# A routed feed-forward phase whose program order is written out by hand on four engines

## The chip, the cores and the metric

The kernel runs on one core of a Trainium2 chip. The time is device microseconds (us) of one execution; for the kernel before it is the median of three runs. A core has five instruction streams that matter here: TensorE (PE, matrix products), VectorE (DVE), ScalarE (ACT), GpSimd (POOL), and SyncE (SP, which here only issues transfers). Each stream runs its instructions in the order in which the built program holds them, and waits on semaphores for the others.

## The reference

The input of the second half is the output of the first: a gated linear attention over 4 batches, 8 heads, 768 steps with 48 channels, whose output is laid out as 3072 rows of 384. Then a mixture of 8 experts, each of which takes exactly 384 rows:

```python
logits = x @ w_gate
flat = logits.flatten()
order = np.argsort(-flat)
for idx in order:
    tok, e = (int(idx) // E, int(idx) % E)
    if assigned[tok] >= 0 or counts[e] >= cap:
        continue
    assigned[tok] = e
    counts[e] += 1
for e in range(E):
    mask = assigned == e
    h = np.maximum(x[mask] @ w1[e], 0.0)
    out[mask] = h @ w2[e]
```

The assignment is greedy over all 24576 logits in falling order, so which expert a row goes to depends on which experts are already full.

## The kernel before

**Two phases.** The attention takes the first 136 us or so. It also computes the logits, every row's best expert, and the rows `x_dram` in HBM from which the experts gather. All its engines follow an order written out by hand (L431), and the change leaves it as it is. The feed-forward phase is everything behind it.

**Routing, one expert at a time.** The kernel does not sort. It finds which expert fills up first and at what logit: `search` (L573) is a search over the bits of that logit in five levels of 7, 7, 6, 6 and 6 bits. A level is a chain through two engines. DVE builds a table `cmp` that compares 3072 digits with all digit values (`compare`, L550), PE adds it up per expert with 24 small products into `rt` (L599, "counts"), DVE compares the counts with what each expert may still take (`g`, L600), PE adds these flags up (L606), DVE takes the maximum `k` (L608) and the next digit `nd` (L611). After the fifth level the full expert `es` is known, and `weights` (L526) has SP load its two weight matrices, 3 MB in four transfers. Two small products (L632, L633) give running offsets, `extract` (L704) makes a one-hot table `hot` (L721), PE turns it into row numbers (24 products, L733), DVE writes `idx` (L735), and POOL issues three indirect transfers of 128 rows each into `xr` (L740). `update` (L641) then takes the full expert out and gives each row its next best choice: `top`, the first table of the next search, `chu`, `o`, `rem`. Seven of the eight experts are searched for; the last is what is left (`search_last`, L683).

**The products.** They are done in pairs of rounded float32 pieces. `split` (L757) has ACT write the upper part `whi` of a block of weights and POOL the rest `wlo` (L768); a block is 128 of the 1024 hidden columns, seven blocks of buffers are there. `prep` (L778) turns the gathered rows on PE (L792), ACT keeps the upper part `xh` (L795), DVE the rest `xl` (L797). `ffn1` (L802) is nine products of 128x384 into `h` (L808), followed by `hh` on ACT (L812) and `hl` on DVE (L813); `ffn2` (L818) is nine products into three `y` tiles (L828). So each expert has 144 products, 72 in each half, and the phase 1152. The last block's `y` goes through ACT to `yt` (L832) and POOL scatters it to the output (L839), three indirect transfers per expert.

**What sets the order around the change.** In the feed-forward phase the kernel before does not fix the order. The loop at L859 declares the work expert by expert, and a scheduler places each instruction on its engine by priority. The kernel steers it with priorities (`route`, L848, runs at high priority) and with `issue_after` edges: transposes of an expert come after block 5 of the previous one (`prep`, L786), and in the first expert after some idle-time products `spin_after` on zeros (L561, counts 6, 4, 2, 2). The lines of `BEHIND` (L15) make a POOL split wait until a certain table of the search is done.

**Positions.** In this text, a position is the number of the 1152 products that PE's stream holds ahead of an instruction.

## Time and profile before

| what | value |
|---|---|
| runs | 444.43, 446.31, 446.60 us, median 446.31 |
| profiled execution | 441.98 us |
| its span, first to last instruction | 440.3 us |
| PE busy | 402.0 us, 91% of the span |
| DVE busy | 285.3 us, 65% |
| POOL busy | 273.8 us, 62% |
| ACT busy | 195.9 us, 44% |
| mean granted TensorE clock | 0.951 |

The profiled execution is 1.7 us longer than its span, and 4.3 us (1.0%) shorter than the median of the runs. The profile has several views: a table of busy time by stretch of the span with the granted clock, the list of waits (which engine waited for whom, total, times, longest), the timeline of one engine with the idle time before a row in square brackets and what ended it, and the chain of work that ended last. Matmuls are pipelined, so a row's duration is longer than the distance from its start to the next start; where a product is priced, it is by that distance.

### The profile page before, as it was taken

Reading aid. Unit: us, or ns where it says so; the run is one execution under the profiler, and the core shown is the slowest. Engines: PE = TensorE matmul, PEld = TensorE weight load, DVE = VectorE, ACT = ScalarE, POOL = GpSimd, SP = SyncE. Lnnn points to the kernel's source line nnn. Section 1 sums busy time; section 2 is a strip of 40 time slices with the busy share of each in tenths; the row PEclk is TensorE's granted clock in tenths of the full one; section 3 lists DMA queues with packets and bytes.
Section 4 is the critical chain, followed back from the end, with each engine's and each line's share of the span. In section 5 each row is a group of like instructions: output and inputs, shape, how many; then the busy total and the mean of one; then the engine's idle time right before and its main releaser. Section 6 shows DMA issues by size and latency. Waiting matters only on the chain.

```text
span 440.3 us, 10854 instructions
## 1 busy us (share of the span) xinstructions
PE 402.0 (91%) x4142; PEld 350.9 (80%) x4142; DVE 285.3 (65%) x838; ACT 195.9 (44%) x447; POOL 273.8 (62%) x303
## 2 busy tenths in 40 slices
PE   7999998989897569997998999999999999899993
PEld 3687776768676439987998899799889889799993
DVE  7788888879636665565677777767668677422210
ACT  2377576556564343144226125315415424545411
POOL 4668988677610062745568766774785786798702
PEclk8599999999999856998999899999999999999999
DMA  8999976660006654092055146127118109910101
GB/s 278 320 262 259 245 207 197 180 194 3 2 3 215 220 192 146 1 312 72 13 186 172 41 131 210 55 91 251 55 46 290 63 6 325 348 56 0 56 2 54
DMA packets 34468, 63.40 MB, mean 144 GB/s; under 512 B 3328, under 2 KB 14592, under 8 KB 34416
## 3 DMA queue, kind: packets, MB, share of 16 engines
q1 hardware_dynamic: 28176, 48.54, 36.0%
q0 software_dynamic: 3072, 9.44, 6.6%
q10 hardware_dynamic: 3168, 4.72, 3.1%
q8 instruction: 33, 0.54, 0.5%
q14 instruction: 19, 0.16, 0.1%
HBM read 53.25 MB, written 9.44 MB: 142 GB/s over the span
## 4 chain that ended last, share of the span: by engine, by line
PE 61%; DVE 12%; issue 8%; DMA 7%; POOL 5%; ACT 4%; POOLq 0%; SPq 0%; ACTq 0%; DVEq 0%
PE h L808 16%; PE y L828 14%; PE rt L599 5%; PE y L310 5%; PE y L304 4%; PE s L255 4%; POOL wlo L768 3%; DMA xr<-x_dram,idx 3%; DVE cmp L550 3%; PE xt L247 3%; PE xt L792 2%; PE st L323 2%; PE st L277 2%; DMA w2r<-in_moe_w_dram 2%; DVE sc L219 2%
## 5 line engine op out<-in xcount | busy, mean ns | idle before, releaser
L768 POOL TENSOR_TENSOR wlo<-w2r,whi 128x384 fp32r<-128x384 f32 x64 | 64.9, 1014 | 26.5 <-DVE cmp L550 25.2
L812 ACT ACTIVATE hh<-h 128x384 fp32r<-128x384 f32 x64 | 31.4, 490 | 96.2 <-PE h L808 94.2
L768 POOL TENSOR_TENSOR wlo<-w1r,whi 128x384 fp32r<-128x384 f32 x64 | 64.7, 1012 | 10.7 <-ACT whi L762 4.7
L740 POOL DMA_INDIRECT xr<-x_dram,idx x24 | 29.3, 1219 | 61.5 <-DVE scr L657 31.1
L828 PE MATMUL y<-wlo,hh 128*128 128x384 f32 x192 | 66.9, 349 | 0.0
L828 PE MATMUL y<-whi,hh 128*128 128x384 f32 x192 | 66.6, 347 | 0.0
L828 PE MATMUL y<-whi,hl 128*128 128x384 f32 x192 | 65.4, 341 | 0.0
L813 DVE SCALAR_TENSOR_TENSOR hl<-h,hh 128x384 fp32r<-128x384 f32 x64 | 35.4, 554 | 41.4 <-ACT hh L812 40.8
L762 ACT ACTIVATE whi<-w1r 128x384 fp32r<-128x384 f32 x64 | 32.2, 522 | 52.9 <-PE y L828 36.4
L267 POOL TENSOR_SCALAR_AFFINE_SELECT sm<-sm 128x512 f32<-128x512 f32 x48 | 29.4, 636 | 32.9 <-ACT sm L263 32.9
L808 PE MATMUL h<-xl,whi 128*128 128x384 f32 x192 | 48.6, 354 | 0.0
L808 PE MATMUL h<-xh,wlo 128*128 128x384 f32 x192 | 47.7, 348 | 0.0
L808 PE MATMUL h<-xh,whi 128*128 128x384 f32 x192 | 46.2, 350 | 1.2 <-ACT xh L795 1.2
L839 POOL DMA_INDIRECT out_dram<-yt,idx x24 | 28.4, 1184 | 27.0 <-ACT yt L832 22.2
L288 ACT ACTIVATE sb<-st,sc 128x48 f32<-128x48 f32 x80 | 24.6, 331 | 36.5 <-DVE st L295 21.2
L550 DVE TENSOR_TENSOR cmp<-nd,iota 128x1536 bf16<-128x1536 bf16 (+4 forms) x32 | 38.2, 1203 | 0.8
L599 PEld LDWEIGHTS <-cmp 128*128 128x128 bf16 x816 | 30.4, 118 | 9.8 <-DVE cmp L550 8.3
L828 PEld LDWEIGHTS y<-wlo,hh 128*128 128x128 f32 x192 | 36.7, 191 | 0.0
L828 PEld LDWEIGHTS y<-whi,hl 128*128 128x128 f32 x192 | 36.6, 191 | 0.0
L808 PEld LDWEIGHTS h<-xh,whi 128*128 128x128 f32 x192 | 34.1, 193 | 3.1 <-ACT xh L795 2.9
L828 PEld LDWEIGHTS y<-whi,hh 128*128 128x128 f32 x192 | 36.5, 190 | 0.0
L599 PE MATMUL rt<-o,cmp 128*128 128x8 bf16 x816 | 32.8, 175 | 3.9 <-DVE cmp L550 3.8
(171 smaller groups left out, 807.7 us busy)
## 6 DMA issues: line engine op xcount, KB each, us to landing
w1r<-in_moe_w_dram SPq DMA_DIRECT2D x16, 768.0 KB, 5.7
w2r<-in_moe_w_dram SPq DMA_DIRECT2D x16, 768.0 KB, 7.6
vt<-in_v_dram SPq DMA_DIRECT2D x24, 256.0 KB, 5.6
x_dram<-xg ACTq DMA_DIRECT2D x6, 768.0 KB, 3.7
raw_a<-in_alpha_dram SPq DMA_DIRECT2D x19, 226.2 KB, 5.8
raw_k<-in_k_dram SPq DMA_DIRECT2D x19, 224.0 KB, 5.4
raw_q<-in_q_dram SPq DMA_DIRECT2D x19, 224.0 KB, 6.1
raw_a<-in_alpha_dram SPq DMA_DIRECT2D x5, 258.5 KB, 5.0
```

The source lines that it names most:

```text
L267: nc.gpsimd.affine_select(SM[s][:, h], SM[s][:, h], pattern=[[0, 4], [1, C]], compare_op=OP.is_ge, fill=0.0, base=0, channel_multiplier=-1)
L288: nc.scalar.activation(SB[s, u][:, :D], St[p], AF.Copy, scale=ac)
L550: x = nc.vector.tensor_tensor(words(dst, nt, js), keyed(d, nt, js), each(iotas[t], nt, js), op=OP.is_ge)
L599: nc.tensor.matmul(cnt, cmp[:, j // U, :, j % U], o[:, j], start=(j == 0), stop=(j == NU - 1))
L740: last_gather[0] = nc.gpsimd.indirect_dma_start(out=XR[i][:, b], out_offset=None, in_=x_dram, in_offset=bass.IndirectOffsetOnAxis(ap=IDX[i ...
L762: nc.scalar.activation(hi[:, 0], a, AF.Copy)
L768: y = nc.gpsimd.tensor_sub(lo[:, h], x, hi[:, h])
L808: nc.tensor.matmul(o, a[:, 0, d], x[:, d], start=(n == 0), stop=(n == 3 * DB - 1))
L812: nc.scalar.activation(hh, o, AF.Relu)
L813: nc.vector.scalar_tensor_tensor(hl, o, 0.0, hh, op0=OP.max, op1=OP.subtract)
L828: F2[i, q] = nc.tensor.matmul(Y[b], a[:, bs], w[:, 1].rearrange("p a b -> p (a b)"), start=(q == 0 and n == 0), stop=(q == FB - 1 and n == 2))
L839: st_ = nc.gpsimd.indirect_dma_start(out=out, out_offset=bass.IndirectOffsetOnAxis(ap=IDX[i][:, b:b + 1], axis=0), in_=yt, in_offset=None)
```

## The change

All of the feed-forward phase after the first search is put under a manual schedule: DVE, PE, ACT and POOL run their instructions in the order in which the code declares them. The functions are cut into steps (`counts`, `reached`, `flags`, `next_digit`, `table`, `find`, `offsets`, `places`, `one_hot`, `index`, `gather`, `take_places`, `gone`, `best_left`, `new_choice`, `left`, `split_hi`, `split_lo`, `rows`, `rows_lo`, `scatter`), and each step gets a position. `products` yields one product after another, and before each product the steps whose position has come are declared. The arithmetic is the same. What else differs: `ffn1` takes its nine products in the order upper-upper, lower-upper, upper-lower, so that `xl` is read last; the first `ffn1` of an expert from the third on is put ahead of the last `ffn2` of its predecessor; the first expert's second and third transposes go to the `y` tiles; there are 26 spin products instead of 14, sixteen of them in one run behind the first row numbers; and each scatter has a one-element memset ahead of it on POOL.

```diff
-WARM_IN_ROUTE = (6, 4, 2, 2)
+SPIN = (16, 0, 4, 3, 3)
+TRI = 11
+HOT = 24
...
     def ffn1(i, q):
...
-        for a, x in ((hi, XH[i]), (hi, XL[i]), (lo, XH[i])):
+        for a, x in ((hi, XH[i]), (lo, XH[i]), (hi, XL[i])):
...
+    def products():
+        units = []
+        for i in range(E):
+            mine = [(ffn1, i, q) for q in range(FB)]
+            for q in range(FB - 2):
+                mine.insert(3 + 2 * q, (ffn2, i, [q]))
+            if i < E - 1:
+                mine += [(ffn2, i, [q]) for q in range(FB - 2, FB)]
+            else:
+                mine.append((ffn2, i, list(range(FB - 2, FB))))
+            if i > 1:
+                units.insert(len(units) - 1, mine.pop(0))
+            units += mine
...
+    def level(base, i, t, xl=None):
+        at(base, counts, t)
+        for b in xl or ():
+            at(base, rows_lo, i - 1, b)
+        at(base, reached, t)
+        at(base + 2, flags, t)
+        if t < nb - 1:
+            at(base + 2, next_digit, t)
+            at(base + 2, table, i, t + 1)
...
+    def found(base, i, end):
+        at(base, find, i)
+        at(base + TRI, offsets, i)
+        at(base + TRI, places, i)
+        at(base + HOT, one_hot, i, 1)
+        at(base + end, index, i)
+
+    def renewed(base, i):
+        at(base, take_places, i)
+        at(base, gather, i)
+        at(base + 1, best_left, i)
+        at(base + 6, gone)
...
+    with tc.manual_schedule(engines={E_.DVE, E_.PE, E_.Activation, E_.Pool}):
+        find(0)
+        offsets(0)
+        places(0)
+        one_hot(0, 2)
+        index(0)
+        take_places(0)
+        gone()
+        spin_more(SPIN[0])
+        gather(0)
+        best_left(0)
+        left(0)
+        new_choice(0)
+        table(1, 0)
+        for q in range(4):
+            split_hi(0, q)
+        for n in range(3):
+            split_lo(0, n)
+        spin_more(SPIN[1])
+        rows(0, 0)
+        counts(0)
+        rows_lo(0, 0)
+        reached(0)
+        spin_more(SPIN[2])
+        rows(0, 1)
+        flags(0)
+        next_digit(0)
+        table(1, 1)
...
+        spin_more(SPIN[3])
+        rows(0, 2)
+        rows_lo(0, 1)
+        rows_lo(0, 2)
+        spin_more(SPIN[4])
+
+        base = 0
+        levels(0, 1, {1: 1, 2: 9, 3: 21, 4: 36}, {})
+        found(39, 1, 37)
...
+        base = 76
+        for i in range(1, E):
+            loose = i > 2
+            offs = {0: 35, 1: 52, 2: 68, 3: 84, 4: 100} if loose else {0: 33, 1: 49, 2: 64, 3: 79, 4: 94}
+            end = 144 if loose else 133
+            renewed(base, i) if i < E - 1 else at(base, gather, i)
+            if i < E - 2:
+                at(base + 8, table, i + 1, 0)
...
+            at(base + 31, rows, i, 0)
+            at(base + (48 if loose else 45), rows, i, 1)
+            at(base + (60 if loose else 57), rows, i, 2)
+            if i < E - 2:
+                levels(base, i + 1, offs, {0: (0,), 1: (1,), 2: (2,)})
+                found(base + offs[4] + 3, i + 1, end - offs[4] - 3)
...
+            if i > 1:
+                for b, p in enumerate((56, 72, 88)):
+                    at(base + p, scatter, i - 2, b)
```

Three places show how the instructions now stand. The first is DVE behind the first expert's row numbers, where the first table of the second search is built (`cmp`, 128x3072). Before:

```order
L661 TENSOR_TENSOR scr<-scr,masks 128x120
L675 TENSOR_TENSOR rem<-rem,rt 128x8
L663 TENSOR_SCALAR top<-scr 128x24
L550 TENSOR_TENSOR cmp_98<-top,iota 128x3072
L797 TENSOR_TENSOR xl<-xt,xh 128x3x128
L666 SCALAR_TENSOR_TENSOR scr<-scr,scale 128x96
L671 TENSOR_TENSOR val<-val,scr 128x192
```

And now:

```order
L753 TENSOR_SCALAR top<-scr 128x24
L775 TENSOR_TENSOR rem<-rem,rt 128x8
L776 SCALAR_TENSOR_TENSOR rem<-scr,rem 128x8
L761 TENSOR_TENSOR val<-val,scr 128x192
L762 TENSOR_SCALAR scr<-asg 128x24
L764 TENSOR_REDUCE ch<-val 128x24
L767 SCALAR_TENSOR_TENSOR scr<-scr,scale 128x96
L769 TENSOR_TENSOR chu<-ch,scr 128x24
L771 TENSOR_TENSOR o<-scr,chu 128x192
L552 TENSOR_TENSOR cmp_98<-top,iota 128x3072
L824 TENSOR_TENSOR xl<-xt,xh 128x3x128
L619 TENSOR_TENSOR g<-rt,rem 128x8
```

The table came ahead of the new choices and now comes behind all of them. Of the `xl` steps only the first stands ahead of the level's `g`.

The second is PE around the first two levels of the fourth search (`y` are the second halves of the products, `h` the first; `xt` the transposes; a group of counts is 24 pairs like the last two rows). Before, the first level's flags and the second level's counts:

```order
L792 MATMUL xt<-ident,xr 128x128 x2
L606 LDWEIGHTS one_83
L606 MATMUL rt<-g,one_83 128x8
L792 MATMUL xt<-ident,xr 128x128
L808 MATMUL h<-xh,whi 128x384 x6
L599 LDWEIGHTS cmp_99
L599 MATMUL rt<-o,cmp_99 128x8
```

And now, in the same search:

```order
L855 MATMUL y_3398<-whi,hh 128x384
L855 MATMUL y_3398<-wlo,hh 128x384
L855 MATMUL y_3398<-whi,hl 128x384
L835 MATMUL h<-xh,whi 128x384 x2
L818 MATMUL xt<-ident,xr 128x128 x3
L835 MATMUL h<-xh,whi 128x384
L835 MATMUL h<-xh,wlo 128x384 x3
L614 LDWEIGHTS cmp_99
L614 MATMUL rt<-o,cmp_99 128x8
```

Before, six products stood between the counts of the first two levels, and some transposes with them; now sixteen do in the third and fourth search, seventeen from the fifth on, and the flags stand two products behind the counts. The transposes are at a fixed place among them.

The third is POOL behind a gather (`xr`), where the split of the weights (`wlo`) and the scatters (`out_dram`) share the engine. Before:

```order
L740 DMA xr<-x_dram,idx 128x384 x3
L768 TENSOR_TENSOR wlo<-w1r,whi 128x384
L768 TENSOR_TENSOR wlo<-w2r,whi 128x384
L768 TENSOR_TENSOR wlo<-w1r,whi 128x384
L839 DMA out_dram<-yt,idx 3072x384 x3
L768 TENSOR_TENSOR wlo<-w2r,whi 128x384
```

And now:

```order
L799 TENSOR_TENSOR wlo<-w1r,whi 128x384
L871 MEMSET apart 1x1
L872 DMA out_dram<-yt,idx 3072x384
L799 TENSOR_TENSOR wlo<-w2r,whi 128x384
L799 TENSOR_TENSOR wlo<-w1r,whi 128x384
L871 MEMSET apart 1x1
L872 DMA out_dram<-yt,idx 3072x384
```

The three scatters stood in one run ahead of the fourth split; now there is one scatter behind the splits of each level.

More of the change, by code (lines that the diff above doesn't have):

```diff
@@ L559, in gla_moe_kernel @@
     last_k = [None]
[L561 to L571 removed]
     def search(i):
         chu, o, dig = st["chu"], st["o"], st["dig"]
[L575 to L577 removed]
+        st["d"] = dig[0]
         for t, bits in enumerate(BITS):
[L579 to L581 removed]
+            if t == 0:
                 g = g0
@@ L638, in search @@
[L638 to L648 removed]
+        st["es"] = es
@@ new lines, in index, with gather @@
+    def index(i):
+        ix = psx.tile([128, NB], F32, name="xt")
+        for j in range(NU):
+            nc.tensor.matmul(ix, st["hot"][:, j // U, :, j % U], st["rhs"][:, j], start=(j == 0), stop=(j == NU - 1))
+        IDX[i] = rw.tile([128, NB], I32, name="idx", bufs=4)
+        st["ix"] = ix
+    def gather(i):
+        nc.vector.tensor_scalar(IDX[i], st["ix"], float(N // 2), None, op0=OP.add)
+        XR[i] = wp.tile([128, NB, Dm], F32, name="xr")
+        for b in range(NB):
+            g = nc.gpsimd.indirect_dma_start(
+                out=XR[i][:, b], out_offset=None, in_=x_dram,
+                in_offset=bass.IndirectOffsetOnAxis(ap=IDX[i][:, b:b + 1], axis=0))
+        for half in second_half:
+            for d_ in half(1):
+                tc.add_manual_dep(d_.ins, g.ins.name,
+                                  mybir.DependencyInfo(mybir.DependencyClass.Sync, mybir.DependencyReason.DATA),
+                                  reason="rows of the first expert before its later weights")
+        second_half.clear()
```

470 lines of the change are left out of this document (250 added, 220 removed).

## The prediction

> **What bounds the kernel now.** I read the clock and busy time by stretch first, since the change touches only what comes after 136 us, then the list of PE's waits, then single engines around the gaps. The page says PE is the bound:
>
> ```profile
> PE 402.0 (91%) x4142; PEld 350.9 (80%) x4142; DVE 285.3 (65%) x838; ACT 195.9 (44%) x447; POOL 273.8 (62%) x303
> ```
>
> The stretches of the feed-forward phase (length, then PE, weight loads, DVE, ACT, POOL busy, then granted clock) show where PE was not at work, or at work on a slow clock:
>
> ```profile
> 150.00:167.00 17.00, 9.38 (x76) 5.81 (x75) 11.87 (x43) 5.45 (x13) 7.46 (x6) 0.55 0.63 190
> 167.00:173.00 6.00, 6.00 (x28) 5.52 (x27) 3.24 (x6) 2.40 (x6) 1.65 (x2) 0.58 0.62 228
> 195.00:206.00 11.00, 7.98 (x43) 7.33 (x42) 6.07 (x16) 6.27 (x16) 6.43 (x7) 0.84 0.38 124
> 206.00:234.00 28.00, 27.74 (x277) 26.10 (x276) 19.36 (x63) 9.16 (x21) 16.49 (x17) 1.00 0.38 134
> 234.00:250.00 16.00, 14.06 (x130) 12.22 (x129) 12.11 (x26) 6.15 (x14) 13.96 (x12) 0.89 0.23 77
> 280.00:330.00 50.00, 48.08 (x450) 44.24 (x449) 36.12 (x110) 17.18 (x37) 36.15 (x35) 1.00 0.30 101
> 330.00:375.00 45.00, 44.12 (x390) 41.28 (x390) 33.73 (x110) 19.51 (x43) 31.03 (x29) 1.00 0.52 173
> 375.00:385.00 10.00, 8.50 (x69) 7.65 (x68) 3.79 (x7) 5.46 (x13) 7.70 (x8) 1.00 0.97 359
> 385.00:433.00 48.00, 47.94 (x277) 46.81 (x275) 10.04 (x18) 18.66 (x41) 29.62 (x31) 1.00 0.09 28
> ```
>
> Length less PE's busy time is 3.0, 0.3, 1.9, 1.9, 0.9, 1.5 and 0.1 us from the third row on, 9.6 us in all. The clock adds to it: at half clock half of the time is lost. Three stretches have it: 167 to 173 (some 2.5 us lost: 6.00 x 0.42), 195 to 206 (11.00 x 0.16 is 1.8, of which part was idle anyway; I take 1.5) and 234 to 250 (16.00 x 0.11 is 1.8; 1.5). Who made PE wait:
>
> ```profile
> PE xt L792 <- DMA xr<-x_dram,idx: 5.6, 4, 2.5
> PE rt L599 <- DVE cmp L550: 3.8, 7, 0.9
> PE xt L792 <- DVE xl L797: 2.2, 4, 0.9
> ```
>
> Gathered rows that come late (the longest, 2.5 us, is the gap at 197), and tables of the search that come late. So PE has about 15 us to win behind 167 us, 9.6 idle, 2.5 and 3.0 on clock, and no more than that without less work for it.
>
> **The change, part by part.** *Prices.* A product at full clock is 1.56/9 = 0.173 us:
>
> ```profile
> 387.72 1.56 PE h L808 x9
> ```
>
> A level costs PE its counts and its flags, by the distances of starts:
>
> ```profile
> 251.51 0.96 PE L599 MATMUL rt<-o,cmp 128*128 128x8 bf16 x24
> 252.33 0.42 PE L828 MATMUL y<-wlo,hh 128*128 128x384 f32 x1
> 252.59 0.34 PE L828 MATMUL y<-whi,hl 128*128 128x384 f32 x1
> 252.77 0.18 PE L606 MATMUL rt<-g,one 128*128 128x8 bf16 x1
> 252.81 0.42 PE L828 MATMUL y<-whi,hh 128*128 128x384 f32 x1
> 253.07 0.34 PE L828 MATMUL y<-wlo,hh 128*128 128x384 f32 x1
> ```
>
> Counts take 0.82, the product behind them 0.26 in place of 0.17, flags 0.04 and again 0.09: 1.03 us a level. None of this work goes away; the change has the same 1152 products, the same searches and gathers. It only moves when they are asked for.
>
> *The start of the phase.* The rows of DVE and PE behind the first row numbers:
>
> ```profile
> 156.14 0.16 DVE L735 TENSOR_SCALAR idx<-xt 128x3 int32<-128x3 f32 x1 [0.27 <-PE xt L733]
> 158.39 0.17 DVE L663 TENSOR_SCALAR top<-scr 128x24 bf16<-128x24 int32 x1
> 158.60 1.76 DVE L550 TENSOR_TENSOR cmp<-top,iota 128x3072 bf16<-128x3072 bf16 x1
> 166.12 0.97 PE L599 MATMUL rt<-o,cmp 128*128 128x8 bf16 x24
> 166.95 1.63 PE L808 MATMUL h<-xh,whi 128*128 128x384 f32 x4
> 169.44 1.76 DVE L550 TENSOR_TENSOR cmp<-nd,iota 128x3072 bf16<-128x3072 bf16 x1
> 184.79 0.23 DVE L614 SCALAR_TENSOR_TENSOR fl<-rt,k,ramp 128x8 f32<-128x8 f32 x1
> ```
>
> Before, the first table was ready at 160.36, but its counts stood behind three transposes and came at 166.12; the next table ended at 171.20, and the expert was found at 184.8. Now eight more steps of DVE come ahead of the table. As an estimate they take 2 us (ten such steps took 2.46 us from 156.14 to 158.60), so it ends at 158.6 + 2 + 1.76, about 162.4; but its counts stand right behind the first transpose and start there, 3.7 us sooner. The next table needs 5.1 us from counts to its end above; with the flags behind four spins instead of five cold products I take 4.4: it ends at 166.8. The remaining levels are 8, 12 and 15 products apart, 1.4, 2.1 and 2.6 us plus 1.03 each, the first of them short of the chain (priced below at 3.3 us), so 3.3 + 3.1 + 3.6, and then three products and flags: the expert is found near 177.5, some 7 us before 184.8. The first product needs the third transpose and moves only from 166.95 to about 165.8. At 177.5 PE has done 39 products and all levels; in the trace it had done 35 and lacked two levels. That is 4 x 0.17 + 2 x 1.03 = **2.7 us**, with the half clock of 167 to 173 already in it.
>
> The bounds of this term come from the clock. If it stays at 0.5 as in the row of 167 to 173, the 2.5 us lost there are lost again and 0.2 remain. The row that speaks for full clock is the gap at 197: PE took up work at 199.81, and the clock per microsecond, 0.60 from 202 to 203 and 1 behind it, came back at 202.8, after 3.0 us without a pause (the rows of 243 and 247 are the edges of the other slow stretch):
>
> ```profile
> 199.81 0.87 PE L792 MATMUL xt<-ident,xr 128*128 128x128 f32 x3 [2.51 <-DMA xr<-x_dram,idx]
> 199.00:200.00 1.00, 0.19 (x1) 0.70 0.46 158
> 202.00:203.00 1.00, 1.00 (x5) 0.60 0.00 0
> 243.00:244.00 1.00, 0.91 (x25) 0.88 0.00 0
> 247.00:248.00 1.00, 0.70 (x4) 0.91 0.00 0
> 155.97 2.08 PE L569 MATMUL h<-warm 128*128 128x384 bf16 x6
> ```
>
> Sixteen spins at 2.08/6 = 0.35 us or a little less are 5 us without a pause, more than that, so I take full clock from 162 us on.
> [...]
>
> *The gaps at 195 and 234.* The first is the second expert's gather, late because its search was. With that search 7 us earlier and the transposes 31 products (5.4 us) behind the row numbers, the rows are there. A later gather shows what 5.4 us has to cover:
>
> ```profile
> 231.54 0.16 DVE L735 TENSOR_SCALAR idx<-xt 128x3 int32<-128x3 f32 x1 [0.19 <-PE xt L733]
> 235.54 0.52 PE L792 MATMUL xt<-ident,xr 128*128 128x128 f32 x3 [0.78 <-DMA xr<-x_dram,idx]
> ```
>
> 4.0 us from `idx` to rows, with weights in flight. The second gap is DVE and POOL in each other's way:
>
> ```profile
> 245.12 2.86 DVE L550 TENSOR_TENSOR cmp<-nd,iota 128x1536 bf16<-128x1536 bf16 x1
> 250.36 0.95 DVE L550 TENSOR_TENSOR cmp<-nd,iota 128x1536 bf16<-128x1536 bf16 x1
> 245.19 1.01 POOL L768 TENSOR_TENSOR wlo<-w2r,whi 128x384 fp32r<-128x384 f32 x1
> ```
>
> A table of 0.95 took 2.86 us while POOL ran splits that three scatters in a row had pushed back. With one scatter behind each level's splits that doesn't come up. I take both gaps as gone: 3.0 + 0.3 + 1.9 idle and 1.5 + 1.5 clock, **8.2 us**. Below, if the rows are late by the 0.78 above in each of seven experts, 5.5 us come back.
>
> *The waits between 280 and 385.* The waits for tables (1.9 + 0.9) are of the same kind; and from 375 on, with the transfers' share at 0.97, the last expert's weights (3 MB) met the gather before. Now the last but one gather stands 12 products ahead of the last expert's search, and the last gather 194 products ahead of its use. **4.3 us**.
>
> *New waits.* A level's chain is set by DVE, which also does `hl` (554 ns in the mean) between the products' halves:
>
> ```profile
> L813 DVE SCALAR_TENSOR_TENSOR hl<-h,hh 128x384 fp32r<-128x384 f32 x64 | 35.4, 554 | 41.4 <-ACT hh L812 40.8
> 248.04 0.96 PE L599 MATMUL rt<-o,cmp 128*128 128x8 bf16 x24 [0.34 <-DVE cmp L550]
> ```
>
> From these counts to the end of the table at 250.36 + 0.95 = 251.31 it is 3.3 us with one `hl` in it. Fifteen or sixteen products and a level are 3.6 to 3.8 us, so they cover it. From the first level to the second the table is the 1.76 us one and an `xl` (about 0.5) stands ahead: 3.3 + 0.8 + 0.5 = 4.6 against 16 x 0.173 + 1.03 + three transposes (an estimate, 0.3) = 4.1: 0.4 us short in five searches, **2 us** of new waits. The bounds: none, if `hl` falls elsewhere; 0.4 at each of the 25 later levels, 10 us.
>
> Spins, memsets and the new order inside `ffn1` I cost at nothing. The spins end by about 161.5 (5 us from 156.3), and the table that PE needs next only at 162.4; were the table there at once, they would cost up to 1 us. The memsets are covered by POOL's idle third, and `xl` last only gives slack. The last scatters, 433 to 440.3, stay.
>
> **The sum.** 2.7 + 8.2 + 4.3 - 2 = 13.2 us off the profile's 441.98: 428.8. The median of the runs is 1.0% above that execution, so I put 446.31 x 428.8/441.98 = **433 us**.
>
> **The rivals.** *(a) The clock stays low at the start.* For it: the wait ahead of the first row numbers, in which the clock fell (0.55 in the row of 150), is still there, and 14 spins did not lift it before. Against: those stood in four runs of 6, 4, 2 and 2. The row of 199 makes it the less likely. [...] It costs the 2.5 us: 435.5.
>
> *(b) The fixed order makes PE wait at each level.* An engine with a fixed order waits where a scheduler would have put something else in between, and 0.4 us at each of 25 levels is 10 us in place of 2: 441. Against: before, the distance was 6 to 15 products, and most levels there had no wait.
>
> *(c) The gaps only move.* If gathers and weights collide at the new place as at 197 (2.5 us in four of seven experts, 10 us) and the clock stays low at the start too (2.5), 0.7 of the 13.2 us are left: 444 to 448, no change. Against: the spacing of 31 products.
>
> *(d) Slower.* One mechanism: the chain of a level is longer than its spacing by 0.7 us at all 25 levels, since each `hl` between two steps of the search must now wait for its product. That is 17.5 us in place of 2, and idle time within a search can let the clock fall as at 244, which cost 1.5. It decides from 0.6 us per level (15.2/25); at 0.7 and with two such falls it gives 452. For it: in DVE's new order two or three `hl` of 0.55 us stand inside each search. Against: by their positions most have their product behind them already.
>
> **How the numbers follow.** The forecast has 0.50, (a) 0.14, (b) 0.15, (c) 0.08, (d) 0.10; 0.03 are for more than I found, such as waits too short to show as idle time (424 or less). The range of 424 to 445 leaves out most of (d), a part of (c) and the last case. A measurement of this kernel tells 0.5% (444.1 to 448.5) from no change. Faster: 0.50 + 0.14 + 0.15 + 0.03 = 0.82; the same: 0.08; slower: 0.10.
>
> **What would show it.** Right: the second search's `fl` at 176 to 179 and PE's first product near 166; no idle row above 1 us for gathers behind 180; full clock from 162 or 165 on and no fall behind it; tables of 0.95 and 1.76 us, none near 2.9; the chain of waits with products at its core to the end. Wrong: waits of counts for `cmp` or of flags for `g` above 5 us in all (b, d); rows of gathers above 4 us in all (c); a clock of 0.5 until 169 or 172 (a).

## The result

| kernel | median | range of its runs | before beside it | ratio, 95% interval |
|---|---|---|---|---|
| changed, first chip | 434.21 us | 433.69 to 435.52 | 446.21 us | 0.974 (0.971 to 0.978) |
| changed, second chip | 434.43 us | 432.73 to 437.54 | 446.09 us | 0.975 (0.971 to 0.980) |
| changed, third chip | 436.23 us | 433.61 to 437.19 | 445.71 us | 0.979 (0.976 to 0.983) |

The change makes the kernel faster by 9.5 to 12 us. The forecast was 433 us. The profiled execution took 433.69 us, its span is 431.8 us, and its mean granted clock is 0.969. So the two profiled executions are 8.3 us apart, 13.2 had been summed. Of the experiments below, two of ten runs of "offsets later" (441.07 and 441.46 us) and one of four of "levels 8 apart" (464.32 us) took over 1.5% longer than the fastest run of the same kernel and are left out of the medians and ranges.

### The profile page after: what moved, and what is told of

Same layout as the page of the kernel before. It is cut to its first block, busy times and chain, and to the rows that moved or that the text cites. A ratio compares the mean times of both kernels' runs of the same rounds, so it can differ in the third digit from the quotient of the medians.

```text
span 431.8 us, 10887 instructions
## 1 busy us (share of the span) xinstructions
PE 396.6 (92%) x4154; PEld 347.8 (81%) x4154; DVE 284.2 (66%) x838; ACT 195.7 (45%) x447; POOL 279.9 (65%) x327
## 4 chain that ended last, share of the span: by engine, by line
PE 62%; DVE 21%; issue 6%; DMA 4%; POOL 3%; ACT 2%; SPq 0%; DVEq 0%; POOLq 0%; ACTq 0%
PE h L835 17%; PE y L855 16%; PE rt L614 6%; PE y L312 4%; PE y L306 4%; PE s L257 4%; DVE ga L226 3%; DVE sc L221 2%; DVE cmp L552 2%; PE xt L344 2%; DVE hot L699 2%; PE xt L249 2%; DMA raw_a<-in_alpha_dram 2%; PE xt L818 2%; PE xt L708 2%
## 5 line engine op out<-in xcount | busy, mean ns | idle before, releaser
L799 POOL TENSOR_TENSOR wlo<-w1r,whi 128x384 fp32r<-128x384 f32 x64 | 69.2, 1082 | 24.1 <-ACT whi L790 22.4
L799 POOL TENSOR_TENSOR wlo<-w2r,whi 128x384 fp32r<-128x384 f32 x64 | 68.0, 1063 | 25.6 <-PE xt L818 9.5
L855 PE MATMUL y<-whi,hh 128*128 128x384 f32 x192 | 64.9, 338 | 0.0
L835 PE MATMUL h<-xh,whi 128*128 128x384 f32 x192 | 47.5, 346 | 0.1
L835 PE MATMUL h<-xh,wlo 128*128 128x384 f32 x192 | 46.0, 344 | 0.0
L835 PE MATMUL h<-xl,whi 128*128 128x384 f32 x192 | 46.0, 344 | 0.0
L872 POOL DMA_INDIRECT out_dram<-yt,idx x24 | 25.0, 1043 | 18.4 <-ACT yt L859 14.6
L835 PEld LDWEIGHTS h<-xh,wlo 128*128 128x128 f32 x192 | 33.8, 189 | 0.0
L552 DVE TENSOR_TENSOR cmp<-nd,iota 128x1536 bf16<-128x1536 bf16 (+4 forms) x32 | 33.1, 1044 | 1.0
L835 PEld LDWEIGHTS h<-xl,whi 128*128 128x128 f32 x192 | 33.6, 189 | 0.0
```

The source lines that it names most:

```text
L552: x = nc.vector.tensor_tensor(words(dst, nt, js), keyed(d, nt, js), each(iotas[t], nt, js), op=OP.is_ge)
L799: y = nc.gpsimd.tensor_sub(lo[:, h], x[h], hi[:, h])
L835: nc.tensor.matmul(o, a[:, 0, d], x[:, d], start=(n == 0), stop=(n == 3 * DB - 1))
L855: nc.tensor.matmul(Y[b], a[:, bs], w[:, 1].rearrange("p a b -> p (a b)"), start=(q == 0 and n == 0), stop=(q == FB - 1 and n == 2))
L872: st_ = nc.gpsimd.indirect_dma_start(out=out, out_offset=bass.IndirectOffsetOnAxis(ap=IDX[i][:, b:b + 1], axis=0), in_=yts.pop((i, b)), in ...
```

## The profile after, beside the profile before

From the page of the changed kernel, the line of busy time and the line of the granted clock over 40 slices:

```profile
PE 396.6 (92%) x4154; PEld 347.8 (81%) x4154; DVE 284.2 (66%) x838; ACT 195.7 (45%) x447; POOL 279.9 (65%) x327
PEclk9699999999999769999999999999999999999998
```

PE is busy for 5.4 us less, although it has twelve more spins. Behind the 15th slice the clock does not fall until PE is done, in the last. Busy time by stretch of the changed kernel (length, PE, weight loads, DVE, ACT, POOL, granted clock, share and GB/s of the transfers):

```profile
150.00:167.00 17.00, 10.23 (x97) 6.57 (x96) 14.20 (x48) 5.60 (x13) 6.10 (x7) 0.80 0.72 227
167.00:173.00 6.00, 5.62 (x71) 4.83 (x70) 4.29 (x11) 0.89 (x3) 4.01 (x5) 1.00 0.38 141
173.00:195.00 22.00, 20.69 (x196) 19.21 (x195) 17.04 (x59) 8.00 (x19) 15.50 (x15) 1.00 0.50 171
195.00:206.00 11.00, 11.00 (x115) 10.11 (x114) 6.83 (x15) 5.16 (x12) 5.63 (x6) 1.00 0.01 1
206.00:234.00 28.00, 26.60 (x246) 24.70 (x245) 22.86 (x70) 10.69 (x25) 19.77 (x19) 1.00 0.38 135
234.00:250.00 16.00, 14.93 (x144) 13.68 (x143) 9.93 (x37) 7.34 (x17) 12.93 (x16) 1.00 0.25 85
250.00:280.00 30.00, 29.58 (x288) 27.35 (x287) 22.05 (x66) 11.98 (x27) 23.51 (x24) 1.00 0.35 122
280.00:330.00 50.00, 49.82 (x455) 46.79 (x454) 38.99 (x117) 20.09 (x45) 35.81 (x34) 1.00 0.47 162
330.00:375.00 45.00, 41.48 (x352) 38.97 (x350) 26.00 (x84) 18.25 (x41) 33.27 (x39) 1.00 0.54 189
375.00:385.00 10.00, 10.00 (x60) 9.75 (x59) 3.05 (x6) 6.32 (x15) 9.43 (x14) 1.00 0.17 62
```

Length less PE's busy time, and what the low clock cost, from 167 us on. The clock of 195 to 250 before is half of the time in which PE was busy at a clock of 0.50: 2.99 us from 199.40 to 202.80 and 3.42 us from 243.76 to 247.18. At that clock products start 0.32 us apart (201.12, 201.44, 201.76, 202.08) against 0.173 at full clock, so 46% of the time is lost, a little less than the half that the table and the prediction take. Of the stretches that the prediction does not show, PE was busy for 22.00 us from 173 to 195 and 30.00 us from 250 to 280.

| stretch | idle before | clock before | idle now | clock now |
|---|---|---|---|---|
| 167 to 195 | 0 | 2.5 | 1.7 | 0 |
| 195 to 250 | 5.2 | 3.2 | 2.5 | 0 |
| 250 to 280 | 0 | 0 | 0.4 | 0 |
| 280 to 385 | 4.3 | 0 | 3.7 | 0 |
| sum | 9.5 | 5.7 | 8.3 | 0 |

15.2 us became 8.3. That is 6.9 of the 8.5 us between the spans; the first product comes 1.3 us sooner (165.65 us against 166.95), which is the rest, to 0.3 or so. So every loss that the forecast wanted gone is gone. What is there now is new: the idle time in the last columns stands at other instructions. PE's waits in the changed kernel (engine, waiting tile and line, what it waited for, total, times, longest), and the rows of PE and DVE that the text speaks of:

```profile
PE xt L708 <- DVE rhs L701: 4.4, 4, 2.9
PE rt L659 <- DVE rts L640: 3.3, 4, 1.3
PE rt L663 <- DVE rts L653: 2.7, 1, 2.7
PE xt L818 <- DMA xr<-x_dram,idx: 1.5, 1, 1.5
PE rt L614 <- DVE cmp L552: 1.3, 3, 0.7
```

```profile
165.65 0.44 PE L835 MATMUL h<-xh,whi 128*128 128x384 f32 x1
185.81 0.34 PE L708 MATMUL xt<-rhs,hot 128*128 128x3 f16 x6 [0.72 <-DVE rhs L701]
213.69 0.16 PE L659 MATMUL rt<-rts,tri 128*128 128x2 bf16 x1 [0.79 <-DVE rts L640]
246.66 0.16 PE L659 MATMUL rt<-rts,tri 128*128 128x2 bf16 x1 [1.07 <-DVE rts L640]
358.19 0.18 PE L663 MATMUL rt<-rts,tri 128*128 128x1 bf16 x1 [2.72 <-DVE rts L653]
```

```profile
178.28 0.23 DVE L628 SCALAR_TENSOR_TENSOR fl<-rt,k,ramp 128x8 f32<-128x8 f32 x1
354.09 0.56 DVE L841 SCALAR_TENSOR_TENSOR hl<-h,hh 128x384 fp32r<-128x384 f32 x1 [1.23 <-issue]
356.42 1.20 DVE L649 TENSOR_TENSOR asg<-asg,chu 128x24 f32<-128x24 f32 x1
357.94 0.19 DVE L653 TENSOR_REDUCE rts<-scr 128x1 bf16<-128x24 f32 x1
```

Waits for tables are down from 3.1 to 1.3 us (the 3.8 us of the kernel before hold 0.7 us of the first search, which has a line of its own now). Waits for gathered rows are down from 5.6 to 2.1: 1.5 ahead of the first product, and 0.6 at 193.06, which this profile puts down to DVE's `rem` and others of the same order to the gathered rows. In their place stand waits for the steps between a search and its row numbers: the running offsets (L659, L663, for `rts`) and the one-hot table (L708, for `rhs`). The first expert's share of these two lines is not new: 1.3 of the 3.3 us and 2.9 of the 4.4, where the kernel before had 1.3 and 3.3. New are 2.1 us for L659 (0.79, 1.07 and 0.22), 1.5 for `rhs` on L708 and 2.7 for L663.

The longest is the last expert's offset at 358: PE has it 20 products behind the last searched expert's row numbers, and DVE gets there 2.72 us later. DVE takes 6.3 us from these row numbers (351.67) to `rts` (357.94). In its chain stand an `hl` that waits for its product (1.23 us without work, until ACT has its `hh` ready at 354.06, and 0.5 of its own) and an addition, `asg`, of 1.20 us.

## The experiments

Twelve runs of ten kernels were made in three jobs, each job on one chip. The kernel before differs from chip to chip (441.81, 446.09 and 445.71 us), so medians are compared within a job. For the first job, in which the changed kernel itself did not run, the kernel "last routing late" is the bridge, since it ran in the first and in the third.

| job | kernel | median | range |
|---|---|---|---|
| 1 | last routing late | 432.44 us | 431.77 to 433.10 |
| 1 | short spins | 436.14 us | 435.30 to 437.60 |
| 1 | scatters in one run | 436.61 us | 436.32 to 437.44 |
| 1 | offsets later | 437.78 us | 434.42 to 440.87 |
| 2 | changed kernel | 434.43 us | 432.73 to 437.54 |
| 2 | last routing late, 16 and 22 spins | 433.21 us | 433.05 to 434.88 |
| 2 | second search late | 445.94 us | 445.05 to 448.95 |
| 2 | levels 8 apart | 457.35 us | 456.00 to 460.79 |
| 3 | changed kernel | 436.23 us | 433.61 to 437.19 |
| 3 | last routing late, again | 432.50 us | 431.47 to 433.76 |
| 3 | last routing late, 16 and 30 spins | 433.05 us | 432.30 to 436.24 |
| 3 | old order in `ffn1` | 434.57 us | 433.60 to 436.12 |

A second yardstick does without medians. In each profile I take the time from the first expert's running offset (the first row of L659) to the second expert's row numbers (L708), "start", and from there to the end of the span, "rest". In the changed kernel's three profiles these are 34.36 and 246.0, 34.34 and 246.0, 36.27 and 246.9 us.

### The last expert's routing, late

```diff
...
-                at(base + 20, offsets, i + 1)
-                at(base + 20, places, i + 1)
-                at(base + 26, one_hot, i + 1, 1)
+                at(base + 40, offsets, i + 1)
+                at(base + 40, places, i + 1)
+                at(base + 46, one_hot, i + 1, 1)
                 end = 40
-                at(base + end, index, i + 1)
+                at(base + 70, index, i + 1)
```

Its gather, transposes and `xl` move 30 products with it.

> Only the last expert's routing is moved: its running offset and places from position 20 to 40 behind the start of expert 7's plan, its one-hot table from 26 to 46, its row numbers from 40 to 70, its gather and transposes 30 products later. Theory (the one new wait that was not priced, 2.72 us of PE for DVE at 358, comes from the position alone): the wait is gone, idle time of PE from 330 to 375 falls from 3.5 us to about 0.8, time 434.2 - 2.7 = 431.5 us (430.8 to 432.3). Rival 1 (the wait only moves to the row numbers or to the gathered rows of the last expert): a row of 1.5 to 3 us for index or for the transposes appears, time 434 to 436. Rival 2 (DVE's chain itself is what is long there, whatever PE does): the products behind it wait for hl or for cmp instead, time 433.5 to 434.5.

It ran again beside the changed kernel:

> The last expert's routing late, the same kernel as in the first experiment, now beside the changed kernel on one chip. Theory (the 2.72 us wait of the last running offset was on the path that sets the end, and of the waits that it leaves behind 0.5 + 0.5 + 0.4 us are new): 1.5 to 2.5 us below the changed kernel, 432.3 where that takes 434.4. Rival (no gain, the first experiment ran on a quicker chip): within 0.7 us of the changed kernel.

It took 432.44 and 432.50 us, in the third job 3.7 below the changed kernel, so a little above the range of the first forecast and more below the changed kernel than the second one had it; rest is 243.9 and 244.1 us against 246.0 to 246.9. The second run's stretch, and the largest wait that is left in it:

```profile
330.00:375.00 45.00, 43.33 (x367) 40.60 (x366) 27.83 (x85) 19.15 (x42) 32.09 (x35) 1.00 0.52 178
360.19 0.52 PE L818 MATMUL xt<-ident,xr 128*128 128x128 f32 x3 [0.53 <-DMA xr<-x_dram,idx]
```

Idle time there is 1.7 us against 3.5: the wait was on the path that sets the end, 2.7 went and about 1 came back in three small pieces. Rival 1 and rival 2 of the first text fall. By rest the gain is 2.0 us against a changed kernel without a fall of the clock and 2.8 against the one of the third job; the 3.7 us between the medians are more than either, and why is not shown. A part is a second price of the wait. In the third job's profile of the changed kernel the clock fell behind it:

```profile
358.00:360.00 2.00, 0.56 (x3) 0.57 (x4) 1.72 (x6) 0.00 (x0) 0.83 (x1) 0.79 0.20 76
360.00:362.00 2.00, 2.00 (x8) 2.00 (x7) 1.86 (x7) 0.00 (x0) 0.00 (x0) 0.50 0.83 300
362.00:364.00 2.00, 2.00 (x13) 1.96 (x12) 1.44 (x4) 1.06 (x3) 0.00 (x0) 0.85 1.05 392
```

It did so in three of six profiles that have this wait at 358 (here, with short spins, and with the scatters in one run), and in neither of the two of this kernel. By the median no other kernel of the study was faster.

### The offsets of every search, later

```diff
-TRI = 11
-HOT = 24
+TRI = 16
+HOT = 29
...
-            end = 144 if loose else 133
+            end = 144 if loose else 138
```

> Only the distance from the end of a search to its running offsets grows, from 11 to 16 products (and with it the one-hot table from 24 to 29, and the row numbers of the third and fourth expert by 5). Theory (the offsets stand too close behind the search, DVE needs about 3 us for them): the waits of offsets (0.79, 1.07 and 0.22 us) go to 0.2 in all, those of the row numbers (0.37 to 0.72, four of them, 1.8 in all) stay where the distance to the offsets is kept and grow by 0.4 each where it shrinks from 25 to 20: 434.2 - 1.9 + 1.2 = 433.5 us (432.5 to 434.2). Rival (the row numbers set the pace, the offsets only take a part of their wait): waits of row numbers grow by as much as those of offsets shrink, 434.2 (433.7 to 435.5).

It took 437.78 us, 5.3 above the kernel with the late last routing, which is 1.6 above the changed kernel if that stands 3.7 above the bridge, as in the third job; rest is 250.0, 4.0 above. The waits for `rts` of L659 did go: of 3.3 us only the first expert's 1.3 are left. Those for `rhs` grew by 0.5 and 0.6 us, near what was forecast. But all that comes later moved by 10 products, and now first halves end right ahead of a level. DVE, then PE, in the sixth search:

```profile
297.66 0.56 DVE L841 SCALAR_TENSOR_TENSOR hl<-h,hh 128x384 fp32r<-128x384 f32 x1 [1.39 <-ACT hh L840]
298.14 0.55 DVE L824 TENSOR_TENSOR xl<-xt,xh 128x384 fp32r<-128x384 f32 x1
298.60 0.15 DVE L619 TENSOR_TENSOR g<-rt,rem 128x8 bf16<-128x8 f32 x1
```

```profile
298.81 0.17 PE L599 MATMUL rt<-g,one 128*128 128x8 bf16 x1 [0.94 <-DVE g L619]
```

`hl` must wait for its products, `xl` and `g` stand behind it, and PE waits 0.94 us for the flags, in three searches alike. Neither the theory nor the rival had this. The rest of the loss is clock: it fell to 0.50 behind waits of 0.98 us (251) and 0.96 (263), and 30 us at a mean of 0.89 from 250 to 280 are 3.3 us. The waits are the mechanism that the prediction's rival (d) named, an `hl` between two steps of the search, and they show that the positions of the changed kernel are good for the place of the halves among them, not for the spacing alone.

The run also takes the 2.72 us wait apart. The last expert's offset stands 20 products behind the row numbers here too, but no `hl` waits in DVE's chain, and `asg` takes 0.17 us:

```profile
357.75 0.15 DVE L713 TENSOR_SCALAR idx<-xt 128x3 int32<-128x3 f32 x1
361.62 0.18 PE L663 MATMUL rt<-rts,tri 128*128 128x1 bf16 x1 [0.47 <-DVE rts L653]
```

From row numbers to `rts` (361.37) DVE takes 3.6 us in place of 6.3, and PE waits 0.47 us. So the position alone was short by about 0.5 us; of the 2.7 us by which DVE's chain is longer in the changed kernel, 1.7 are the `hl` and 1.0 is the long `asg`. Moving the step gave room to a long chain, it did not shorten it: with the late last routing DVE still takes 6.3 us.

### The run of spins, short

`SPIN` begins with 6 in place of 16.

> Only the first run of idle-time products is cut from 16 to 6, so 2 us without a pause instead of 4.2. Theory (the long run lifts the clock before the products start): clock 0.5 to 0.6 until about 172, as in the kernel before, 2.5 us lost and the second search later by as much: 434.2 + 2.5 = 436.7 us (436 to 438). Rival (the clock rises anyway with the counts, transposes and spins that follow, or the lost time is hidden because the tables of the search set the pace there): 434.2 (433.7 to 435), even at a low clock.

```profile
160.00:163.00 3.00, 1.67 (x27) 1.30 (x28) 2.12 (x3) 2.71 (x7) 1.56 (x2) 0.50 0.51 149
163.00:167.00 4.00, 3.91 (x24) 2.40 (x21) 2.38 (x5) 1.65 (x4) 2.32 (x3) 0.65 0.61 190
167.00:173.00 6.00, 5.54 (x68) 4.64 (x69) 4.58 (x12) 0.49 (x1) 3.95 (x4) 1.00 0.38 138
```

The clock stays at 0.5 until near 166 and is at 1.00 from 167 on, not from 172. Start is 34.84 us, only 0.5 longer. The median, 436.14, lies in the theory's range, but not for the theory's reason: rest is 248.0, 2.0 above the changed kernel, with the fall of the clock behind the wait at 358. The median is 3.7 above the late last routing, as the changed kernel's is in the third job, so beyond the 0.5 us no loss from the spins can be seen. The rival holds: the clock rises anyway, and what is lost until 166 hardly delays anything. What lifts it, with PE busy for 3.91 of the 4.00 us from 163 to 167, and whether the loss lies under the table, was not tested apart. So the forecast's reason for the full clock, a run of 5 us without a pause, was not needed.

It was not enough either. The third job's profile of the changed kernel, with its 16 spins:

```profile
168.00:174.00 6.00, 6.00 (x41) 5.07 (x40) 3.05 (x8) 1.10 (x3) 3.17 (x4) 0.50 0.06 19
```

The clock was up (1.00 from 163 to 168) and fell again, for 6 us in which PE had no pause; start is 36.27 us, 1.9 longer. This is so in three of the ten profiles whose first run has 16 spins (36.3 to 36.5 us in the other two, both with the late last routing). The longest wait from 156 us to the fall is 0.87 us, ahead of the counts at 166.09. Why the clock falls in some executions of the same first part and not in others is not shown.

### More spins

On top of the late last routing, 16 spins stand ahead of `index(0)`, and 22 or 30 in place of 16 behind it.

> The last expert's routing late, as in the first experiment, and more idle-time products: 16 in PE's wait for the first row numbers, and 22 in place of 16 behind them. [...] Rival 1 (a low clock is hidden there behind tables and gathered rows): clock 1.0, the time that of the first experiment, 432.4 (431.8 to 433.1). Rival 2 (the longer run of spins ends behind the gathered rows): first product 1 us later or more, 433 to 434.

> As the kernel with the late last routing, with 16 idle-time products in PE's wait for the first row numbers and 30 in place of 16 behind them. With 22 PE stood idle for 1.66 us ahead of the gathered rows, and the clock fell right behind, to 0.5 from 163 to 166. Theory (a wait of 1.5 us or more ahead of products is what lets the clock fall; 30 products at full clock are 4.9 us and reach to the rows): no fall from 152 on, idle time for the gathered rows below 0.6 us, 1 to 2 us below the kernel with the late last routing (430.8). Rival 1 (the clock at the start is hidden behind the tables of the second search): the same as that kernel within 0.7 us. Rival 2 (the long run meets a low clock in many executions and is then 9 us long): 2 to 4 us above it, with a wide spread.

With 22, PE had the rows late and the clock fell right there:

```profile
161.43 0.52 PE L818 MATMUL xt<-ident,xr 128*128 128x128 f32 x3 [1.66 <-DMA xr<-x_dram,idx]
162.00:164.00 2.00, 2.00 (x28) 1.44 (x29) 0.00 (x0) 2.00 (x6) 1.84 (x2) 0.67 0.12 48
164.00:166.00 2.00, 1.99 (x9) 1.26 (x8) 1.46 (x5) 0.67 (x2) 1.09 (x2) 0.50 0.82 222
```

With 30 it did not fall: the profile has a clock of 1.00 from 156 on and a mean of 0.984. But start is 34.94 and 35.30 us, no better than the 34.3 of a changed kernel without a fall, and the times are 433.21 and, beside 432.50 for the same kernel without them, 433.05 us. Rival 1: the clock of this stretch is largely hidden. DVE's chain sets the pace there: with 30 spins and a full clock PE waits for DVE four times, at 161.69, 164.24, 166.73 and 169.72 (0.42, 0.60, 0.47 and 0.38 us). More spins cannot shorten that.

### The scatters in one run

`enumerate((56, 72, 88))` becomes `enumerate((54, 54, 54))`: all three scatters of an expert are issued behind the second level's table, ahead of the splits.

> Only the three scatters of an expert are put in one run again, ahead of the splits of the second level (position 54 in place of 56, 72 and 88). Theory (spreading the scatters is what ended the tables of 2.4 to 2.9 us): POOL's splits run into the next table, a table of 2 us or more and a wait of counts of about 1.5 us appear in each of the four searches that have scatters, and the clock falls in one or two of them: 434.2 + 6 = 440 us (438 to 442). Rival (POOL's spare third takes the run, since its splits now have a place of their own): no table above 1.3 us among those of 128x1536, waits of counts below 1 us in all, 434.2 (433.7 to 435).

From the groups by line and shape, one table in DVE's timeline, PE's wait for it, and the clock later on:

```profile
L552 DVE TENSOR_TENSOR cmp<-nd,iota 128x1536 bf16<-128x1536 bf16 x14 | 19.6, 1404 | 0.4
232.04 2.96 DVE L552 TENSOR_TENSOR cmp<-nd,iota 128x1536 bf16<-128x1536 bf16 x1
235.06 0.96 PE L614 MATMUL rt<-o,cmp 128*128 128x8 bf16 x24 [0.81 <-DVE cmp L552]
360.00:366.00 6.00, 6.00 (x21) 5.90 (x21) 3.96 (x10) 1.80 (x4) 0.84 (x1) 0.52 0.95 345
```

The mean of the fourteen tables of 128x1536 is 1404 ns; in the changed kernel it is 962, in the kernel before 1340. Four of them, one in each search with scatters, take 2.37 to 2.96 us. So such tables do come from the run of scatters that pushes the splits into the next level: on POOL the last scatter ends at 232.16 here, and two splits run from 232.18 to 234.17, beside the table. But PE felt it once in the profile, by 0.81 us, because the levels are 15 to 17 products apart. Rest is 250.2, 4.2 above the changed kernel; 2.9 of that is the fall of the clock behind the wait at 358 (6.00 us at 0.52), so about 1.3 us are the scatters. The time, 436.61, is 4.2 above the late last routing, which is 0.5 to 2 above the changed kernel, if that stands 2.0 to 3.7 above the bridge. The mechanism of the theory is right, its price of 6 us is not.

### The levels closer

```diff
-            offs = {0: 35, 1: 52, 2: 68, 3: 84, 4: 100} if loose else {0: 33, 1: 49, 2: 64, 3: 79, 4: 94}
+            offs = {t: (35 if loose else 33) + 8 * t for t in range(5)}
...
```

The `xl` and the end of each search stay at their old positions.

> Levels of the third to seventh search 8 products apart in place of 15 to 17; everything else, the end of each search too, stays at its position. Theory (a level's chain is 3.3 us, and 4.6 from the first to the second): 8 products and a level are 2.4 us, so each search waits 2.2 + 3 x 0.9 = 4.9 us, five searches 24 us, as waits of counts for cmp: 434.2 + 24 = 458 us (452 to 462). Rival (the chain has become much shorter than 3.3 us, since DVE puts it ahead of hl, xl and new choices; that is why no waits came): waits of counts below 8 us in all, 436 to 442.

```profile
PE rt L614 <- DVE cmp L552: 12.5, 16, 2.0
206.00:250.00 44.00, 37.72 (x344) 34.28 (x343) 29.41 (x82) 14.20 (x32) 25.79 (x25) 0.97 0.28 95
250.00:280.00 30.00, 27.32 (x221) 25.11 (x221) 21.09 (x65) 11.46 (x26) 20.79 (x21) 0.90 0.37 132
280.00:330.00 50.00, 47.42 (x410) 43.23 (x409) 30.75 (x93) 18.52 (x42) 31.74 (x35) 0.91 0.29 100
330.00:375.00 45.00, 43.17 (x365) 39.70 (x364) 30.70 (x95) 17.05 (x39) 31.14 (x31) 0.92 0.42 141
```

457.35 us, 2.8% (2.0 to 3.5) slower than the kernel before by the means of the runs, and 22.9 above the changed kernel: the sum of the theory held, half of its working did not. Waits for tables are 12.5 us, not 24: 1.2 to 2.0 from the first level to the second, but only 0.2 to 0.4 at most later ones (1.45 and 1.33 in the fourth search, where two tables took 2.32 and 1.93 us instead of 0.96). The other half is clock: 44 x 0.03 + 30 x 0.10 + 50 x 0.09 + 45 x 0.08 = 12.4 us. A level's chain is thus shorter than 3.3 us. It can be read in the changed kernel, from the counts of a level to the end of the next table:

```profile
267.83 0.96 PE L614 MATMUL rt<-o,cmp 128*128 128x8 bf16 x24
269.80 0.96 DVE L552 TENSOR_TENSOR cmp<-nd,iota 128x1536 bf16<-128x1536 bf16 x1
```

That is 2.9 us (267.83 to 270.76), and 3.7 from the first level to the second (259.29 to 263.02), where 4.6 had been summed; the next counts come at 271.68, so 0.9 us are to spare. Waits in the searches and falls of the clock behind them are the two prices of the prediction's rival (d); here they come from a spacing that the change does not have, not from an `hl` between the steps.

### The second search late

```diff
-        levels(0, 1, {1: 1, 2: 9, 3: 21, 4: 36}, {})
-        found(39, 1, 37)
+        levels(0, 1, {1: 19, 2: 33, 3: 45, 4: 59}, {})
+        found(69, 1, 40)
...
-        base = 76
+        base = 109
```

The third and fourth search are drawn together (12 products a level, row numbers at 121) to catch up.

> The second search is put back to where it stood in the kernel before: counts at positions 19, 33, 45 and 59, row numbers at 109, transposes of the second expert at 127, 133 and 139; the two searches behind it are drawn together so that from the fourth expert on all stands at most 9 products later. Theory (the gap at 195 and the fall of the clock behind it come from this late search): rows of the second gather late by about 2.5 us, a fall of the clock of 3.4 us behind it (1.5 lost), and 2 us of waits for row numbers and tables in the drawn-together searches: 434.2 + 6 = 440 us (438 to 443). Rival (the gap came from weights that were in flight, not from the search's place): no row above 1 us for gathered rows, 434.2 to 437.

445.94 us: 1.001 (0.999 to 1.004) of the kernel before, so the whole gain is gone; theory and rival both had less. In order DVE's row numbers of the second expert, POOL's first gather, PE's first transpose, the stretch, and the last expert's row numbers:

```profile
190.72 0.16 DVE L713 TENSOR_SCALAR idx<-xt 128x3 int32<-128x3 f32 x1 [1.04 <-PE xt L708]
194.98 2.31 POOL L716 DMA_INDIRECT xr<-x_dram,idx  x1
199.49 0.87 PE L818 MATMUL xt<-ident,xr 128*128 128x128 f32 x3 [5.32 <-DMA xr<-x_dram,idx]
195.00:206.00 11.00, 6.41 (x50) 5.77 (x50) 4.94 (x13) 3.00 (x7) 4.18 (x3) 0.84 0.19 56
374.70 0.93 PE L708 MATMUL xt<-rhs,hot 128*128 128x3 f16 x24 [2.94 <-DVE xl L824]
```

The gap and the fall of the clock behind it are back: 4.6 us idle and 1.8 on clock. But the experiment is not clean. POOL issued the gather 4.3 us behind the row numbers, since I had left the first splits of the second expert's weights ahead of it, and these weights come later with a late search; and the 2.94 us at 374 come from where I put the last row numbers. An estimate from the rows: the gathered rows came 4.5 us behind the first gather here (194.98 to 199.49) and 5.2 in the kernel before (194.65 to 199.81); issued right behind the row numbers, at 190.9, it would have brought them at 195.4 to 196.1, when PE had waited since 194.2. So a late search brings back a gap at 195, but by this estimate only 1 to 2 of the 5.3 us are its own. How much of the 11.5 us is the search alone, and how much the order around it, stays open.

### The order in ffn1

The three kinds of products of a first half go back to upper-upper, upper-lower, lower-upper.

> Only the order of the nine products of a first half is put back: upper-upper, upper-lower, lower-upper, so that xl is read from the fourth product on. Theory (costed at nothing: xl stands at a fixed place of DVE's order 15 products or more ahead of its reader, except in the first expert): at most one wait of 0.5 us for xl in the first expert, within 0.7 us of the changed kernel. Rival (xl last is what keeps PE from waiting for DVE): waits for xl of 0.3 to 0.5 us in most of eight experts, 2.5 to 4 us above the changed kernel.

434.57 us beside 436.23 us, so 1.7 below where 0.7 at most was expected, but the runs overlap (433.60 to 436.12 and 433.61 to 437.19). Start and rest are 34.34 and 246.1 us, as in the changed kernel without a fall of the clock, and no wait for `xl` stands in front of a first half. Costed at nothing, and by the profile nothing it is.

### The changed kernel again

> The changed kernel itself once more, beside the kernel before on the chip of this job, since the kernel before took 446.2 us beside it at first and 441.8 us beside the first four experiments. Theory (before differs from chip to chip by how often its clock falls, the changed kernel does not, since it leaves no gaps in which it falls): 434.2 us again (433.5 to 435.5), whatever before takes. Rival (the whole chip is 1% quicker or slower): the ratio stays at 0.974, so about 430 where before takes 441.8.

> The changed kernel again, as the measure for the other runs of this job. By its first two jobs: 434.3 us (433 to 436), and 0.975 of the kernel before on the same chip (0.970 to 0.980).

It stayed at 434 to 436 us on three chips, while the kernel before had 446.21, 446.09, 445.71 and, beside the first four experiments, 441.81. The kernel before does vary in clock between executions (0.941 to 0.963 over three jobs), but so does the changed one (0.953 to 0.973). How the changed kernel runs on the chip where the one before takes 441.81 was not tried, so neither the theory nor the rival of the first text is decided.

## Why the prediction was right, and where it was not

The time was right by 0.3%, the sum less so: 428.8 us were summed for the profiled execution, and 433.69 came out. The 433 came out because the profile of the kernel before was one of its quick executions, 1.0% under its median, and the changed kernel's only 0.1%; two errors of 4 to 5 us met. That the time is right to 0.3% is luck; that most of the losses named go, and about 12 us with them, is not.

*The start, 2.7 us.* The first product was due near 165.8 and came at 165.65, `fl` at 177.5 and came at 178.28, the 2.5 us of slow clock are gone in this profile, and 1.7 us of new waits came up. In three of ten profiles the clock fell here after all, at a price of about 2 us, which is rival (a) in those executions. The reason given, the long run of spins, was not needed: with a run of 6 the clock is up near 166, and start is 0.5 us longer.

*The gaps at 195 and 234, 8.2 us.* 5.2 idle and 3.2 of clock are gone, 8.4 in all, and 2.5 of new waits came up. In this profile no gathered rows are late by more than 0.6 us behind 180, and no table of 128x1536 takes longer than 1.02 us. That the run of scatters stretches the tables was shown; that this alone cost PE much was not: with wide levels it costs 1 to 2 us. The first gap comes back with a late search, as far as an unclean experiment can show it; by the estimate above 1 to 2 us of it are the search's own.

*The waits from 280 to 385, 4.3 us.* All gone, and 3.7 us of others came. The waits for tables among them went with the wider levels rather than with the scatters: with the scatters in one run the tables of the fifth to seventh search take 2.4 us again, and PE does not wait for them. The waits from 375 on were not tested apart.

*New waits, 2 us.* This step failed. They are 8.3 us, and most of them at other places than those looked at. The levels, where 0.4 us in five searches were expected, wait 0.24 us in all behind the second search, because the chain of a level is 2.9 us and not 3.3, and from the first level to the second 3.7 and not 4.6. The steps between a search and its row numbers were not priced at all: running offsets 0.8 + 1.1 + 0.2, one-hot tables 0.7 + 0.4 + 0.4 + 0.3, and the last expert's offset, 2.7. Positions times 0.173 us against a chain of rows, as it was done for the levels, would have shown that the last offset is short by about 0.5 us. The other 2.2 would have needed the `hl` and the long `asg` in DVE's chain, and of these the `hl` is what rival (d) named, at the one place where nobody looked.

*The rivals.* (b) and (c) did not come. (d) did not come at the levels because their spacing has about 1 us to spare, and its prices are real: levels 8 products apart cost 23 us, an `hl` ahead of a level 0.95 us a search, and an `hl` in the last expert's chain holds DVE up for 1.7 us ahead of the wait at 358.

## What to carry to other kernels

When an order is written out by hand, price every place where one engine hands over to another, the rare ones (the last expert, the end of a search) too: the step repeated 25 times had been given its room, the one that stands there once had not, and moving it was worth 2 us or more, while more spins gained nothing. Price the chain with all that an engine with a fixed order does between its steps: one instruction whose input comes late holds up everything behind it, as the `hl` at 354.09 did with 1.23 us without work on DVE. A wait on the bounding engine has two prices here, its length and the clock that may fall behind it, as it did behind the 2.7 us at 358 in three of six profiles. Before a wait is moved by shifting all that follows, look at which other steps come to stand together.

## What was not expected of the hardware

The clock fell for 6 us (0.50 from 168 to 174) while PE was busy without a pause, 2 us behind a wait of 0.87 us (166.09), and a fall came there in three of ten executions of the same first part. Behind a wait of 2.7 us it fell in three of six, and with the offsets later it fell behind waits of 0.98 and 0.96 us.

An addition of 128x24 (`asg`, L649) took 1.20 us, where its neighbours take 0.14 to 0.36. In eleven profiles splits run on POOL beside it; it takes 1.20 to 1.24 us in each and ends with a split. In the other two (offsets later, second search late) POOL issues a gather at that time, and it takes 0.17, as in the kernel before (L689). So the long time goes with the splits beside it. It is no rule for every small addition: one of the same shape (L636) takes 0.18 us in each search, at 278.41 for one, with a split on POOL from 277.96 to 278.97. What sets the two apart is open.
